# Softmax biases and part of P's high halves on ACT in place of DVE

## The chip, the core and the metric

The kernel runs on one core of a Trainium2 chip. The metric is the device time of one execution in microseconds (us); the figure given for a kernel is the median of its runs. A core has engines with instruction queues of their own, each worked off in order: PE (TensorE, matmuls; PEld is its weight load), DVE (VectorE), ACT (ScalarE), POOL (GpSimd) and SP (SyncE), which here issues most DMAs and all DMA transposes. Engines wait for each other by semaphores.

## What is computed

Three blocks, one after the other. Block-masked attention over 8 batches, 8 heads, 576 positions and a head width of 64; then a dense gated layer over its 4608 tokens; then a routed layer of 8 experts that each take the 576 tokens with the highest logits in one global greedy order.

```python
scores = scale * np.matmul(q, k.transpose(0, 1, 3, 2))
scores = np.where(block_i >= block_j, scores, -1000000000.0)   # blocks of 64
scores = scores - np.max(scores, axis=-1, keepdims=True)
attn = np.exp(scores)
attn = attn / (np.sum(attn, axis=-1, keepdims=True) + 1e-09)
x = np.matmul(attn, v)                       # then (B*S, H*D) = (4608, 512)
a, b = x @ w1, x @ w2                        # 512 -> 1024
x = (a * b @ w3) @ w_out                     # 1024 -> 512
...                                          # greedy assignment of tokens to experts
out[mask] = np.maximum(x[mask] @ w1[e], 0.0) @ w2[e]
```

The change touches the attention's softmax alone: the subtraction of the row maximum, which enters the exponential as a bias, and the division by the row sum.

## The kernel before

All matmuls keep about 32-bit precision by splitting a number into a high and a low fp16 half: the high half is the rounded product, the low half is what the rounding left. A product then takes three matmuls (high x high, high x low, low x high).

The attention is worked through in 32 steps n, one for each pair of heads of a batch. A step has four score tiles S in PSUM (two buffers), made by PE: `last` (L239, the last 64 rows of both heads, 576 keys), and three by `rows` and `mm` (L200, L204): query block 3 (512 keys, both heads), blocks 2 and 0 (384 and 128 keys, both heads), and block 1 (256 keys, both heads). Each tile goes through `finish`:

- DVE takes the row maxima of the scores (L213 for two heads at once, L215 for `last`) into `nb[:, 0]`.
- One DVE instruction multiplies them by minus the scale and writes the biases `nb[:, 1]` (L217; 1, 2 or 4 numbers per partition).
- ACT forms E = exp(scale x S + bias) and the row sums (L221), one instruction for each part.
- DVE turns the sums into reciprocals `rr` (L224, L225).
- For each part the high half of P = E x rr is written in fp16 (L229 on DVE or L231 on ACT), and DVE forms the low half (L232), which reads the high one.

So a step has four biases and nine parts: one of 576 keys and two each of 512, 384, 256 and 128. `N // P` is 4 for 576 and for 512 keys; `DVE_HI = (2, 3, 4)` puts the high halves of all but the 128-key parts on DVE. P lies in two SBUF tiles with one buffer each: P13 (`last` and block 3) and P12 (blocks 2, 0 and 1). SP transposes each by DMA into PT (L259), PE multiplies it with v (L276, `pv`), and ACT and DVE take the result out as xT (L280, L281).

Into these steps other work is woven, by the lists `fills`: the first dense layer's weights are decoded from 64-bit numbers and split in steps 1 to 7 (`decode`, L385 on ACT and L386 to L390 on DVE, then L126, L118, L119), w_out and w3 are prepared in steps 8 to 30, and 128 units of the dense layer (`moe_unit`: 24 matmuls at L301, ACT L306, DVE L311, a store by SP) begin with step 5, four a step. Then come the rest of the dense layer, the routing and the experts.

In the attention part the order on each engine is not that of the code: a scheduler that knows dependencies, buffers and a cost for every instruction lays all queues out when the kernel is built. An edit in one place can therefore move instructions elsewhere. The routing part has a fixed order.

Of the kernel before, what the change touches and what calls it, by code (L numbers as in the profile page):

```python
# [12 lines left out]
AF = mybir.ActivationFunctionType  # L13
ALU = mybir.AluOpType
# [15 lines left out]
R3 = 2  # L30
LE = 37
SW = 30
DVE_HI = (2, 3, 4)
TH = 5
TB = 15
TBX = 5
# [23 lines left out]
def moe_kernel(ctx, tc, q, k, v, moe_w1, moe_w2, moe_w3, moe_w_out, w_gate, ew1, ew2, out):  # L60
    nc = tc.nc
    P = 128
# [128 lines left out]
    def s_tiles(n):  # L191
        tq, tk, t4, c = qkT[n]
        pa_, pc_ = (x[n % PB] for x in Pb)

        def mm(ps, o, m):
            N = (m + 1) * P
            for a, b in PRODUCTS:
                for hh in range(2):
                    r = slice(64 * hh, 64 * hh + 64)
                    nc.tensor.matmul(ps[:, hh, o:o + N], tq[r, a, m * P:m * P + P], tk[r, b, :N],  # L200
                                     start=a + b == 0, stop=False)
            for hh in range(2):
                r = slice(64 * hh, 64 * hh + 64)
                nc.tensor.matmul(ps[:, hh, o + N - 64:o + N], hide[r], low[r], start=False, stop=True)  # L204

        def finish(ps, parts):
            nb = sm.tile([P, 3, 4], F32, name="nb", bufs=8)
            e = c2.tile([P, 2, 512], F32, name="E", bufs=3)
            ef, pf_ = (x.rearrange("p a b -> p (a b)") for x in (e, ps))
            k_ = 0  # L210
            for hh, o, N, _, _ in parts:
                if hh == 0:
                    nc.vector.tensor_reduce(nb[:, 0, k_:k_ + 2], ps[:, :, o:o + N], axis=AX.X, op=ALU.max)  # L213
                elif hh is None:
                    nc.vector.tensor_reduce(nb[:, 0, k_:k_ + 1], pf_[:, :N], axis=AX.X, op=ALU.max)  # L215
                k_ += 1
            nc.vector.tensor_scalar(nb[:, 1, :k_], nb[:, 0, :k_], c[:, 1:2], None, op0=ALU.mult)  # L217
            sums = sm.tile([P, 4], F32, name="sums", bufs=8)
            at = [slice((hh or 0) * 512 + o, (hh or 0) * 512 + o + N) for hh, o, N, _, _ in parts]
            for x, a in enumerate(at):  # L220
                nc.scalar.activation(ef[:, a], pf_[:, a], AF.Exp, bias=nb[:, 1, x:x + 1], scale=c[:, 0:1],  # L221
                                     accum_out=sums[:, x:x + 1])
            r = sm.tile([P, 2, 4], F32, name="rr", bufs=8)
            nc.vector.tensor_scalar(r[:, 0, :k_], sums[:, :k_], 1e-9, 2.0 ** -TS, op0=ALU.add, op1=ALU.mult)  # L224
            nc.vector.reciprocal(r[:, 1, :k_], r[:, 0, :k_])  # L225
            for x, (_, _, N, dst, b0) in enumerate(parts):
                hi, lo = (dst[:, z].rearrange("p b c -> p (b c)")[:, b0 * P:b0 * P + N] for z in range(2))
                if N // P in DVE_HI:
                    nc.vector.tensor_scalar(hi, ef[:, at[x]], r[:, 1, x:x + 1], None, op0=ALU.mult)  # L229
                else:  # L230
                    nc.scalar.activation(hi, ef[:, at[x]], AF.Copy, scale=r[:, 1, x:x + 1])  # L231
                nc.vector.scalar_tensor_tensor(lo, ef[:, at[x]], r[:, 1, x:x + 1], hi, op0=ALU.mult, op1=ALU.subtract)  # L232

        def last():
            ps = ps_s.tile([P, 2, 512], F32, name="S")
            pf_ = ps.rearrange("p a b -> p (a b)")
            for a, b in PRODUCTS:
                for k0, N in ((0, 512), (512, 64)):
                    nc.tensor.matmul(pf_[:, k0:k0 + N], t4[:, a], tk[:, b, k0:k0 + N], start=a + b == 0, stop=a == 1)  # L239
            finish(ps, [(None, 0, S, pa_, 0)])  # L240

        def rows(*ms):
            def f():
                ps = ps_s.tile([P, 2, 512], F32, name="S")
                parts, o = [], 0
                for m, dst, b0 in ms:
                    mm(ps, o, m)
                    parts += [(hh, o, (m + 1) * P, dst, b0 + hh * (m + 1)) for hh in range(2)]
                    o += (m + 1) * P
                finish(ps, parts)  # L250
            return f

        return [last, rows((3, pa_, 5)), rows((2, pc_, 0), (0, pc_, 6)), rows((1, pc_, 8))]
# [330 lines left out]
    for i in range(nl):  # L584
        n = max(n if i else 0, SW + int(i * (LE - SW) / nl), min(NS + 5, 8 + 2 * (i // 2)) if i % 2 else 0)
# [575 lines left out]
```

## Time and profile before

| | |
|---|---|
| median of 3 runs | 1585.56 us (1579.64 to 1587.46) |
| profiled execution, time | 1581.55 us |
| profiled execution, span from first to last instruction | 1579.8 us |
| busy over the span | PE 1366.2 us (86%), DVE 1077.4 us (68%), ACT 795.2 us (50%), POOL 98.3 us (6%) |
| mean granted TensorE clock | 0.945 of full speed |
| high halves on DVE (L229) | 224 instructions; on ACT (L231) 64 of 128 keys |
| biases (L217) | 128 instructions on DVE |

The shares are means over stages that differ: the attention fills the span from about 13 us to about 757 us. DVE is at 90% or more of a slice in most of the first 500 us, PE from then on. The chain of work that ended last, followed back from the end, reaches only to about 1143 us, so it says nothing of the attention; that has to be read from the busy times by stage and from the waits of each engine. A row of waits names the engine and line that waited, what it was let go by, the total in us, how often, and the longest.

### The profile page before, as it was taken

What the parts mean: (1) busy time and instruction counts of PE and PEld (TensorE: products, weight loads), DVE (VectorE), ACT (ScalarE), POOL (GpSimd) and SP (SyncE); (2) the same over time, 40 slices, a digit from 0 to 9 for tenths busy, and PEclk for the clock granted to TensorE, in tenths of its full rate; (3) what the DMA queues carried; (4) which work ended last, traced back from release to release, by engine and by line L of the source; (5) the groups of instructions that cost most, each with busy time, mean ns of one, the idle gap of its engine ahead of it and who ended that gap; (6) DMA issues with size and microseconds to landing.
All of it is one profiled execution on the core that took longest, in us unless ns stands there. A gap on an engine that the chain in (4) does not pass through costs nothing. (4 is left out here: it accounts for less than half of the span.)

```text
span 1579.8 us, 32788 instructions
## 1 busy us (share of the span) xinstructions
PE 1366.2 (86%) x12811; PEld 934.5 (59%) x12811; DVE 1077.4 (68%) x3308; ACT 795.2 (50%) x1881; POOL 98.3 (6%) x136
## 2 busy tenths in 40 slices
PE   3547888789899999999998898879768999999997
PEld 2335656466566666666666665656556656556663
DVE  8999999879888988886115888878743353333610
ACT  7766676566666656544312333353314564655611
POOL 0000000000000000010200000000024121200101
PEclk7559999999999999999999999989879999999999
DMA  7768797887858865559955324332358663642200
GB/s 247 182 148 197 137 232 168 172 200 149 194 136 201 175 169 108 121 114 282 286 172 186 101 81 135 100 120 94 101 112 190 181 199 134 152 149 74 80 27 34
DMA packets 379658, 238.57 MB, mean 151 GB/s; under 512 B 261232, under 2 KB 344688, under 8 KB 378480
## 3 DMA queue, kind: packets, MB, share of 16 engines
q1 hardware_dynamic: 372064, 215.47, 54.2%
q0 software_dynamic: 5760, 18.90, 3.8%
q8 instruction: 100, 1.64, 0.4%
q10 hardware_dynamic: 1680, 2.11, 0.4%
q14 instruction: 54, 0.44, 0.1%
HBM read 132.61 MB, written 39.86 MB: 109 GB/s over the span
## 5 line engine op out<-in xcount | busy, mean ns | idle before, releaser
L301 PE MATMUL ab<-xT,w1h 128*128 128x288 f16 x1536 | 217.6, 290 | 9.0 <-ACT a_sb L306 8.6
L301 PE MATMUL ab<-xT,w2h 128*128 128x288 f16 x1536 | 218.1, 290 | 6.5 <-ACT a_sb L306 2.8
L221 ACT ACTIVATE E<-S,nb,cc 128x128 f32<-128x128 f32 (+4 forms) x288 | 181.2, 639 | 78.3 <-DVE nb L217 52.5
L1079 PE MATMUL pe<-xT,ewa 128*128 128x288 f16 (+2 forms) x1728 | 198.4, 279 | 15.0 <-DMA xT<-xg 10.1
L1079 PEld LDWEIGHTS <-ewa 128*128 128x128 f16 x1728 | 161.2, 101 | 50.8 <-issue 15.4
L1096 PE MATMUL pe<-ewb,h 128*128 128x512 f16 (+1 forms) x960 | 189.1, 379 | 0.0
L301 PEld LDWEIGHTS <-w2h 128*128 128x128 f16 x1536 | 146.3, 100 | 56.1 <-issue 15.8
L301 PEld LDWEIGHTS <-w1h 128*128 128x128 f16 x1536 | 144.8, 99 | 58.3 <-issue 19.3
L276 PE MATMUL PV<-PT,v 128*64 128x128 f16 (+1 forms) x2880 | 100.1, 223 | 66.6 <-DMA PT<-P 55.6
L232 DVE SCALAR_TENSOR_TENSOR P<-E,rr,P 128x128 f16<-128x128 f32 (+4 forms) x288 | 157.3, 572 | 0.4
L1096 PEld LDWEIGHTS <-h 128*128 128x128 f16 (+1 forms) x960 | 85.4, 101 | 99.0 <-issue 2.6
L276 PEld LDWEIGHTS <-v 128*64 128x64 f16 x2880 | 85.1, 118 | 91.0 <-issue 50.6
L1082 DVE SCALAR_TENSOR_TENSOR h<-pe,h 128x288 f16<-128x288 f32 (+2 forms) x144 | 57.1, 420 | 107.6 <-ACT h L1081 107.5
L922 PE MATMUL px<-W34l,gh 128*128 128x512 f32 x288 | 123.6, 429 | 0.0
L922 PE MATMUL px<-W34h,gh 128*128 128x512 f32 x288 | 122.4, 425 | 0.2 <-ACT gh L937 0.2
L922 PE MATMUL px<-W34h,gl 128*128 128x512 f32 x288 | 122.4, 425 | 0.0
L311 DVE SCALAR_TENSOR_TENSOR g<-ab,vr,a_sb 128x288 f32<-128x288 f32 x124 | 65.6, 529 | 69.6 <-PE ab L301 47.5
L306 ACT ACTIVATE a_sb<-ab 128x288 f32<-128x288 f32 x128 | 52.4, 409 | 119.5 <-PE ab L301 111.2
L937 ACT ACTIVATE gh<-g 128x1024 fp32r<-128x1024 f32 x36 | 38.1, 1059 | 142.3 <-PE px L922 135.1
L1081 ACT ACTIVATE h<-pe 128x288 f16<-128x288 f32 (+2 forms) x144 | 52.1, 380 | 108.5 <-PE pe L1079 108.1
L213 DVE TENSOR_REDUCE nb<-S 128x2 f32<-128x1024 f32 (+3 forms) x128 | 101.3, 814 | 4.8 <-PE S L204 4.8
L229 DVE TENSOR_SCALAR P<-E,rr 128x384 f16<-128x384 f32 (+3 forms) x224 | 88.0, 429 | 1.6
(279 smaller groups left out, 2158.6 us busy)
## 6 DMA issues: line engine op xcount, KB each, us to landing
g<-gd SPq DMA_DIRECT2D x36, 512.0 KB, 3.7
gd<-g SPq DMA_DIRECT2D x62, 288.0 KB, 3.4
g<-gd SPq DMA_DIRECT2D x15, 1152.0 KB, 7.6
raw<-in_moe_w_dram SPq DMA_DIRECT2D x32, 512.0 KB, 4.9
esa<-in_moe_w_dram SPq DMA_DIRECT2D x8, 2048.0 KB, 9.2
esb<-in_moe_w_dram SPq DMA_DIRECT2D x8, 2048.0 KB, 8.4
v<-in_v_dram SPq DMA_DIRECT2D x8, 1280.0 KB, 6.9
xr<-row SPq DMA_DIRECT2D x36, 256.5 KB, 3.3
```

The costliest lines, as they stand in the source:

```text
L213: nc.vector.tensor_reduce(nb[:, 0, k_:k_ + 2], ps[:, :, o:o + N], axis=AX.X, op=ALU.max)
L221: nc.scalar.activation(ef[:, a], pf_[:, a], AF.Exp, bias=nb[:, 1, x:x + 1], scale=c[:, 0:1], accum_out=sums[:, x:x + 1])
L229: nc.vector.tensor_scalar(hi, ef[:, at[x]], r[:, 1, x:x + 1], None, op0=ALU.mult)
L232: nc.vector.scalar_tensor_tensor(lo, ef[:, at[x]], r[:, 1, x:x + 1], hi, op0=ALU.mult, op1=ALU.subtract)
L276: nc.tensor.matmul(ps[hh * 64:hh * 64 + 64, c0:c0 + w], vt[:, zv, hh, j, :], s, start=z == 0 and j == 0, stop=z == 2 and j == nj - 1)
L301: nc.tensor.matmul(p[:, :288], w[:, zw, cc, :], x[:, zx, cc, c0:c0 + 288], start=first, stop=cc == 3 and zw == 1)
L306: nc.scalar.activation(a, p[:, :288], AF.Copy, scale=2.0 ** -15)
L311: nc.vector.scalar_tensor_tensor(g, ps["w2"][:, :288], iv[b][:, f:f + 1], a, op0=ALU.mult, op1=ALU.mult)
L922: nc.tensor.matmul(p, gh[a][:, f], W34[b][:, f], start=f == 0 and a + b == 0, stop=f == 7 and a == 1)
L1079: nc.tensor.matmul(p[:, :n], w1[:, a, cc, f * P:(f + 1) * P], t[:, 4 * b + cc, x], start=cc == 0 and a + b == 0, stop=cc == 3 and a == 1)
L1082: nc.vector.scalar_tensor_tensor(h[:, 1, f, x], p[:, :n], 0.0, h[:, 0, f, x], op0=ALU.max, op1=ALU.subtract)
L1096: nc.tensor.matmul(p[r0:r1], h[:, a, f, k_ * P + r0:k_ * P + r1], EW[e, "b"][0][:, b, f], start=f == 0 and a + b == 0, stop=f == 7 and a == 1)
```

## The change

`DVE_HI` becomes two lists, one for steps 0 to 7 and one for steps 8 to 31, and the bias instruction goes from DVE to ACT:

```diff
-DVE_HI = (2, 3, 4)
+DVE_HI = (2,), (2, 3)
...
-            nc.vector.tensor_scalar(nb[:, 1, :k_], nb[:, 0, :k_], c[:, 1:2], None, op0=ALU.mult)
+            nc.scalar.activation(nb[:, 1, :k_], nb[:, 0, :k_], AF.Copy, scale=c[:, 1:2])
...
-                if N // P in DVE_HI:
+                if N // P in DVE_HI[n >= 8]:
                     nc.vector.tensor_scalar(hi, ef[:, at[x]], r[:, 1, x:x + 1], None, op0=ALU.mult)
                 else:
                     nc.scalar.activation(hi, ef[:, at[x]], AF.Copy, scale=r[:, 1, x:x + 1])
```

In each of steps 0 to 7 five high halves go to ACT (one of 576, two of 512, two of 384 keys), in each of steps 8 to 31 three (576, 512, 512). That is 40 + 72 = 112 of the 224, and all 128 biases. The scheduler lays all queues out anew; three places show how.

ACT in step 2 before, where E_653 (576 keys) and E_673 (512) are the exponentials of P13, dec, wd and wp belong to the decoding of weights, and P130 is P13:

```order
L221 ACTIVATE E_653,sums_656<-S_645,nb_652,cc_471 128x576
L118 ACTIVATE w2h1_80<-wd_872,wp_883 128x512
L126 ACTIVATE w1h2_72,wm_1005<-wd_998 128x512
L221 ACTIVATE E_673,sums_676<-S_663,nb_672,cc_471 128x512 x2
L280 ACTIVATE xT_320<-PV_567 128x192
L118 ACTIVATE qkT_977<-qk32_500,qp_982 128x1152 x2
```

The same place of ACT now:

```order
L126 ACTIVATE w2h2_81,wm_1147<-wd_1140 128x512
L385 ACTIVATE dec_1260<-raw_1016 128x512
L385 ACTIVATE dec_1405<-raw_1159 128x512
L221 ACTIVATE E_653,sums_656<-S_645,nb_652,cc_471 128x576
L280 ACTIVATE xT_320<-PV_567 128x192
L217 ACTIVATE nb_672<-nb_672,cc_471 128x2
L221 ACTIVATE E_673,sums_676<-S_663,nb_672,cc_471 128x512 x2
L231 ACTIVATE P130_119<-E_653,rr_658 128x576
L217 ACTIVATE nb_768<-nb_768,cc_471 128x4
L118 ACTIVATE w1h2_72<-wd_998,wp_1009 128x512
L118 ACTIVATE w2h2_81<-wd_1140,wp_1151 128x512
L231 ACTIVATE P130_119<-E_673,rr_679 128x512 x2
```

The high halves stand behind the next exponentials or behind weight splits, and two decodes, which wait for a DMA of raw weights, now stand ahead of E_653.

DVE in the same step before, around the high half of E_653:

```order
L224 TENSOR_SCALAR rr_679<-sums_676 128x2
L229 TENSOR_SCALAR P130_119<-E_653,rr_658 128x576
L281 SCALAR_TENSOR_TENSOR xT_320<-PV_567,xT_320 128x192
L390 SCALAR_TENSOR_TENSOR wd_1140<-raw_891,dec_1141 128x512
L213 TENSOR_REDUCE nb_768<-S_751 128x2 x2
```

And now, from a reciprocal of E_673 to the low half of E_653:

```order
L225 RECIPROCAL rr_679<-rr_679 128x2
L84 TENSOR_SCALAR wp_1151<-wp_1151 128x1
L416 COPY w2i_87<-wp_1151 128x1
L418 SCALAR_TENSOR_TENSOR iw12_88<-w1i_78,wp_1151 128x1
L232 SCALAR_TENSOR_TENSOR P130_119<-E_653,rr_658,P130_119 128x576
```

The L229 between reciprocal and low half is gone, and the low half L232 now waits for ACT's L231.

ACT in step 10 before, where a_sb belongs to units of the dense layer:

```order
L306 ACTIVATE a_sb_3483<-ab_3470 128x288
L221 ACTIVATE E_3363,sums_3366<-S_3355,nb_3362,cc_3142 128x576
L306 ACTIVATE a_sb_3564<-ab_3551 128x288
L221 ACTIVATE E_3383,sums_3386<-S_3373,nb_3382,cc_3142 128x512 x2
L306 ACTIVATE a_sb_3687<-ab_3674 128x288
```

And now:

```order
L217 ACTIVATE nb_3362<-nb_3362,cc_3142 128x1
L221 ACTIVATE E_3242,sums_3245<-S_3232,nb_3241,cc_2349 128x256 x2
L221 ACTIVATE E_3363,sums_3366<-S_3355,nb_3362,cc_3142 128x576
L306 ACTIVATE a_sb_3338<-ab_3325 128x288
L118 ACTIVATE qkT_3848<-qk32_3160,qp_3853 128x1152 x2
L231 ACTIVATE P130_119<-E_3363,rr_3368 128x576
L217 ACTIVATE nb_3382<-nb_3382,cc_3142 128x2
L280 ACTIVATE xT_2887<-PV_3267 128x192
L221 ACTIVATE E_3383,sums_3386<-S_3373,nb_3382,cc_3142 128x512 x2
L306 ACTIVATE a_sb_3413<-ab_3400 128x288
L217 ACTIVATE nb_3529<-nb_3529,cc_3142 128x4
L231 ACTIVATE P130_119<-E_3383,rr_3389 128x512 x2
```

Biases and high halves lie between exponentials and the evacuations of dense units (the units beside a given step are earlier ones now: a_sb_3413 where a_sb_3687 stood).

## Rows read from the trace of the kernel before

**Rows 1.** Busy time by stage: start:end, length, us (instructions) per engine, clock, DMA share.
```profile
core 0: us, PE busy (x) PEld busy (x) DVE busy (x) ACT busy (x) POOL busy (x), PEclk, DMA share, GB/s
13.00:192.50 179.50, 109.50 (x1322) 77.95 (x1318) 171.91 (x506) 122.37 (x299) 0.00 (x0) 0.75 0.75 178
192.50:450.90 258.40, 221.69 (x2609) 156.93 (x2610) 233.09 (x620) 165.18 (x403) 0.00 (x0) 0.97 0.82 182
450.90:757.00 306.10, 289.68 (x3411) 199.72 (x3409) 250.82 (x670) 167.93 (x420) 6.09 (x13) 0.99 0.71 164
```

**Rows 2.** L217 alone in these stages: length, DVE us (instructions), clock, DMA share, GB/s.
```profile
13.00:192.50 179.50, 6.89 (x32) 0.75 0.75 178
192.50:450.90 258.40, 9.31 (x44) 0.97 0.82 182
450.90:757.00 306.10, 10.88 (x52) 0.99 0.71 164
```

**Rows 3.** Waits of DVE from 13 to 192.5 us, the longest in total.
```profile
DVE rr L224 <- ACT E L221: 2.3, 4, 1.3
```

**Rows 4.** Waits of PE from 13 to 192.5 us.
```profile
PE PV L276 <- DMA PT<-P: 33.8, 17, 7.2
PE S L200 <- ACT E L221: 10.7, 10, 3.3
```

**Rows 5.** Waits of SP's DMA queue from 13 to 192.5 us.
```profile
SPq L259 <- DVE P L229: 45.1, 15, 7.5
```

**Rows 6.** Waits of PE from 192.5 to 450.9 us.
```profile
PE PV L276 <- DMA PT<-P: 15.4, 16, 2.0
PE S L239 <- ACT E L221: 7.4, 4, 3.4
PE lgp L469 <- DMA w3h<-wo: 4.9, 4, 2.0
```

**Rows 7.** Waits of PE from 450.9 to 757 us.
```profile
PE PV L276 <- DMA PT<-P: 6.5, 7, 1.9
```

**Rows 8.** Waits of ACT from 13 to 192.5 us.
```profile
ACT dec L385 <- DMA raw<-in_moe_w_dram: 17.0, 9, 4.0
ACT xT L280 <- PE PV L276: 11.0, 5, 3.9
ACT E L221 <- DVE wp L80: 7.3, 3, 4.4
```

**Rows 9.** Instructions by line and shape: count, busy us, mean ns, idle before.
```profile
L229 DVE TENSOR_SCALAR P<-E,rr 128x512 f16<-128x512 f32 x64 | 28.0, 479 | 0.5
L229 DVE TENSOR_SCALAR P<-E,rr 128x384 f16<-128x384 f32 x64 | 24.1, 419 | 0.6
L231 ACT ACTIVATE P<-E,rr 128x128 f16<-128x128 f32 x64 | 22.4, 406 | 4.9 <-issue 2.4 <-DVE rr L225 1.5 <-DVE rr L224 1.0
L229 DVE TENSOR_SCALAR P<-E,rr 128x576 f16<-128x576 f32 x32 | 16.4, 513 | 0.4
```

**Rows 10.** Line L118: ns of one (least/median/most), first and last start.
```profile
L118 ACT ACTIVATE w1h<-wd,wp x8: 715/726/762, 32.7 to 172.0; 128x512 f16<-128x512 f32 x8
L118 ACT ACTIVATE wgxh<-wg,wgxp x1: 326/326/326, 280.2 to 280.2; 128x32 f16<-128x32 f32 x1
```

**Rows 11.** Instructions in order of time, 75 to 99 us: start, us, engine, instruction.
```profile
85.53 0.22 DVE L217 TENSOR_SCALAR nb<-nb,cc 128x2 f32<-128x2 f32 x1
85.66 0.75 DVE L386 TENSOR_SCALAR dec<-dec 128x512 f32<-128x512 f32 x2
...
94.17 0.87 DVE L229 TENSOR_SCALAR P<-E,rr 128x512 f16<-128x512 f32 x2
94.24 0.72 ACT L118 ACTIVATE w2h<-wd,wp 128x512 f16<-128x512 f32 x1
...
94.85 0.56 ACT L221 ACTIVATE E<-S,nb,cc 128x256 f32<-128x256 f32 x1
...
94.96 0.44 DVE L167 TENSOR_SCALAR vr<-iw,vs 128x1 f32<-128x1 f32 x2
```

## The prediction, made before the changed kernel ran

> **What bounds the kernel now.** I read the busy time by stage first, then each engine's waits inside a stage, then what single instructions cost. I cut the attention at the first reduce of steps 0, 8 and 19 and at its end, so that the three stages hold 8, 11 and 13 steps (32, 44 and 52 biases, four a step) [rows 2].
>
> In the first stage, 13.0 to 192.5 us, DVE is busy 171.9 of 179.5 us; ACT has 122.4 and PE 109.5 [rows 1]. The longest total wait of DVE there is 2.3 us, for a row sum [rows 3], so DVE is simply full. What PE waits for most is the transposed P, 33.8 us [rows 4]; and SP, which issues those transposes, waits 45.1 us for DVE's part of P [rows 5]. So PE's wait for PT is largely a wait for DVE, passed on by a DMA.
>
> In the second stage, to 450.9 us, no engine is full: of 258.4 us DVE has 233.1 (90%), PE 221.7 (86%), ACT 165.2 (64%) [rows 1]. PE still waits for PT, 15.4 us, then for exponentials that hold a score buffer, 7.4, and for the transposes of w3 and w_out, 4.9, with which the change has nothing to do [rows 6].
>
> In the third stage, to 757 us, PE is busy 289.7 of 306.1 us [rows 1]. Its longest wait, again for PT, is 6.5 us [rows 7]. What lies behind 757 us has no instruction of the change; I expect its time to stay.
>
> **What the change takes from DVE.** An instruction in a row of others costs less than its own duration, since the next begins before it ends. The bias lasts 0.22 us but the next DVE instruction starts 0.13 us after it (85.53 to 85.66); two high halves of 512 keys begin at 94.17 and what follows begins at 94.96, which is 0.395 each against a duration of 0.479 [rows 9, 11]. With the same 0.08 off, 576 keys cost 0.43 and 384 keys 0.335 [rows 9].
>
> - Steps 0 to 7: 0.43 + 2 x 0.395 + 2 x 0.335 + 4 x 0.13 = 2.41 us a step, 19.3 us in eight.
> - Steps 8 on: 0.43 + 2 x 0.395 + 4 x 0.13 = 1.74 us a step, 19.1 us in the second stage, 22.6 in the third.
>
> **What it gives to ACT.** A scaled copy of 512 numbers from fp32 to fp16 lasts 0.72 us on ACT and the next instruction starts 0.61 us after it (94.24 to 94.85); one of 128 lasts 0.406, so about 0.30 by the same 0.11 [rows 9 to 11]. On a straight line 384 keys cost 0.51 and 576 cost 0.66. No row shows a bias on ACT. The nearest is a scaled copy of 32 numbers, 0.326 us, so 0.22 in a row of others [rows 10]; the lower end is what it cost on DVE, 0.13, the upper 0.33 where the exponential right behind must wait for the whole of it. I take 0.22, the nearest row. Below nothing it can go too: the exponential then follows its bias on its own engine, and some of ACT's waits for a late DVE, such as the 7.3 us that exponentials waited in the first stage [rows 8], would shrink.
>
> - Steps 0 to 7: 0.66 + 2 x 0.61 + 2 x 0.51 + 4 x 0.22 = 3.78 us a step, 30.2 in eight.
> - Steps 8 on: 0.66 + 2 x 0.61 + 4 x 0.22 = 2.76 us a step, 30.4 in the second stage, 35.9 in the third.
>
> The bounds of the bias move the first of these sums by 32 x 0.1 = 3 us either way. [...]
>
> **First stage.** DVE falls to 171.9 - 19.3 = 152.6 us of work and ACT rises to 122.4 + 30.2 = 152.6: the two meet. Neither can be full all the time, since they now hand work to and fro: DVE makes the reciprocal, ACT the high half, DVE the low half. That ACT can take high halves without standing idle is shown by the 128-key ones that it has already: 64 of them had 4.9 us of idle time before them [rows 9]; at that price the 40 moved ones add 3 us at most. What I do not expect to shrink are the 17.0 us in which ACT stood before a decode because raw weights were still on their way [rows 8]; the order even puts two decodes ahead of an exponential now. The 11.0 us that it waited for PV [rows 8] and the DVE waits I let the added work fill. So ACT sets the stage: 152.6 + 17.0 = 169.6 us against 179.5, a gain of 9.9. The ends are a loss (the second rival) and 19.3, DVE's whole relief.
>
> [...]
>
> **Second stage.** DVE 233.1 - 19.1 = 214.0, ACT 195.6, PE 221.7 of 258.4: DVE falls below PE. What can be won is the part of PE's idle 36.7 us that came from late P. I take half of DVE's relief, 9.5 us, between nothing and 19.1: PE would then be 89% busy, less than it reaches in the third stage.
>
> **Third stage.** PE bounds it; ACT at 203.8 of 306.1 us has room. I take 1 us, between nothing and the 6.5 of the PT wait.
>
> **Sum.** 9.9 + 9.5 + 1 = 20.4 us off the profiled execution's 1581.55 gives 1561.2; off the median of the runs, 1585.56, it gives 1565.2. I forecast 1563.
>
> **Rivals.**
>
> *No change: DVE was only the busiest.* PE's waits for PT end with a DMA, and the DMA engines are 75 to 83% busy in these stages [rows 1]; P and PT have one buffer each, so a step's P cannot run ahead of the last step's transposes. For it: PE's longest wait names the DMA. Against it: SP itself waited 45.1 us for DVE [rows 5]. DVE's relief would come back as DVE's waits for ACT, the time would move by some 4 us at most: 1578 to 1585.
>
> *Slower: ACT's queue becomes the bound in steps 0 to 7.* ACT's old idle time, 57.1 us in the first stage, stays because it is spent before instructions that wait while others, ready, stand behind them: decodes for DMAs, exponentials for maxima, now biases for maxima and high halves for reciprocals as well. From the point where more than 179.5 - 152.6 = 26.9 us of it stays, the stage is longer than before. If three quarters stay (42.8), it takes 195.4 us, 16 more; with nothing won later, the time is 1598. If all stays it is 30 more, 1612. For it: 17.0 us of these waits are for DMAs, and the order has decodes ahead of exponentials. Against it: the high halves already on ACT waited little, and waits for DVE are part of the 57.1.
>
> *Larger gain: all relief turns into time.* 19.3 + 19.1 + 6.5 = 44.9 us less: 1537. It needs DVE and ACT both near 95% in the first stage.
>
> **How the numbers follow.** Forecast 0.59, own range 1550 to 1576; no change 0.20; slower 0.14; larger gain 0.07. Half a per cent, about what a measurement of this kernel can tell from no change, is 7.9 us, so faster means under 1577.6. The forecast's own range and the larger gain lie there (0.65, and 0.01 of the no-change case): 0.66. Between the bounds I put the rest of the no-change case and the weak end of the forecast, 0.19; slower has 0.15, its own case and a little of the no-change one. The range, 1546 to 1592, leaves out most of the larger gain and the upper half of the slower case, some 0.14 together, and holds the bounds of the bias.
>
> **What would show it.** Right: step 8's first reduce comes about 10 us earlier, at 180 to 185 us, with ACT near 90% busy before it and DVE below 93%; the second stage is some 10 us shorter with PE near 89%; PE's wait for PT falls in both. The bias on ACT lasts about 0.3 us, the high halves 0.6 to 0.8. Wrong: step 8 begins later than 192.5 us with ACT waiting before L217 or L231, or DVE idle before L232 for the high half by as much as it was relieved; or the stages gain as said and the stage from 450.9 us gives it back, since PE there has 95% to do in any case.

## The result, and the profile after

The changed kernel takes 1590.88 us (median of 17 runs, 1586.78 to 1602.83), the kernel before 1583.36 (17 runs on the same chips): a ratio of 1.0064, 95% interval 1.0043 to 1.0085. It is slower by 0.6%, where 1563 us and a gain were forecast. The profiled execution took 1593.24 us, with a span of 1591.5.

The attention, cut as in [rows 1] at the first reduces of steps 0, 8 and 19 and at its end (start:end, length, then PE, PEld, DVE, ACT and POOL busy, clock, DMA share):

```profile
12.30:192.10 179.80, 112.71 (x1248) 77.95 (x1246) 162.19 (x450) 153.34 (x375) 0.00 (x0) 0.75 0.73 183
192.10:457.00 264.90, 229.20 (x2672) 162.08 (x2674) 211.50 (x524) 192.68 (x473) 0.00 (x0) 0.96 0.78 171
457.00:768.00 311.00, 289.49 (x3413) 202.03 (x3413) 228.71 (x580) 205.29 (x513) 5.92 (x13) 0.99 0.71 164
```

Against [rows 1] the stages changed by +0.3, +6.5 and +4.9 us, so the loss lies behind step 8; in the first stage the forecast gain of 9.9 is missing. The sums of work came about as worked out: ACT has 153.3 us in the first stage (forecast 152.6), DVE lost 21.6 and 22.1 us in the other two (19.1 and 22.6). DVE fell by 9.7 in the first, not 19.3, since the stage now holds other work too: DVE has 450 instructions there, 16 more than the 506 of before less the 72 moved ones, among them 20 of the weights' decode L386 where 18 stood.

PE's waits in the first stage (us in total, times, longest):

```profile
PE S L200 <- ACT E L221: 24.3, 13, 4.8
PE PV L276 <- DMA PT<-P: 16.5, 10, 4.7
PE S L239 <- ACT E L221: 9.4, 5, 3.2
```

The wait for PT halved from 33.8 [rows 4], as forecast, and SP's wait for DVE's high halves fell from 45.1 [rows 5] to 16.8, with 14 of them left on DVE where 54 were:

```profile
SPq L259 <- DVE P L229: 16.8, 5, 6.9
```

But all that SP waited before transposes (L259, whatever released it) hardly fell, from 90 to 84 us: other instructions took the place of DVE's high halves. And the score buffers came free late: L200's wait for an exponential, 10.7 before, is 24.3. DVE is no longer full, it stands 17.6 us; its longest waits are for ACT's decodes and for row sums (2.3 before [rows 3]):

```profile
DVE dec L386 <- ACT dec L385: 5.7, 5, 2.0
...
DVE rr L224 <- ACT E L221: 4.1, 6, 1.3
```

ACT's waits in the first stage shrank against [rows 8]: it is idle for 26.5 us (179.8 less 153.3) in place of 57.1. The decodes' wait for raw weights fell from 17.0 to 7.4, with 4.9 more for those of w_out; new is the bias's wait for its maximum:

```profile
ACT nb L217 <- DVE nb L213: 9.8, 6, 3.5
ACT dec L385 <- DMA raw<-in_moe_w_dram: 7.4, 5, 2.1
...
ACT dec L385 <- DMA raw<-in_moe_w_out_dram: 4.9, 2, 4.1
```

PE's wait for PT from 192.1 and from 457.0 us rose, against 15.4 [rows 6] and 6.5 [rows 7]:

```profile
PE PV L276 <- DMA PT<-P: 20.5, 14, 3.7
...
PE PV L276 <- DMA PT<-P: 8.8, 11, 1.8
```

The single high halves last 0.62 to 0.77 us, as expected, and a bias 0.29 (count, busy us, mean ns, idle before):

```profile
L231 ACT ACTIVATE P<-E,rr 128x512 f16<-128x512 f32 x64 | 42.5, 715 | 4.7 <-DVE rr L225 4.7
L231 ACT ACTIVATE P<-E,rr 128x576 f16<-128x576 f32 x32 | 24.6, 769 | 4.6 <-DVE rr L225 3.2 <-ACT E L221 1.2 <-ACT a_sb L306 0.2
L217 ACT ACTIVATE nb<-nb,cc 128x2 f32<-128x2 f32 x64 | 18.7, 293 | 36.0 <-DVE nb L213 35.9
L231 ACT ACTIVATE P<-E,rr 128x384 f16<-128x384 f32 x16 | 9.0, 619 | 0.0
```

So neither durations nor idle time before the moved high halves explain the loss. The idle time before the biases is long, 76.8 us over all three sizes, but it is old: before the change ACT stood 78.3 us ahead of the exponentials L221, now 2.8. The experiments ask what else explains it: the load on ACT, the hand-off between the engines, or the order of the queues.

### The profile page after: what moved, and what is told of

It reads as the page before. It is cut to its first block, busy times and chain, and to the rows that moved or that the text cites. A ratio compares the mean times of both kernels' runs of the same rounds, so it can differ in the third digit from the quotient of the medians.

```text
span 1591.5 us, 32778 instructions
## 1 busy us (share of the span) xinstructions
PE 1376.4 (86%) x12811; PEld 942.3 (59%) x12811; DVE 1024.5 (64%) x3068; ACT 891.7 (56%) x2121; POOL 98.0 (6%) x136
## 5 line engine op out<-in xcount | busy, mean ns | idle before, releaser
L301 PE MATMUL ab<-xT,w1h 128*128 128x288 f16 x1536 | 223.0, 295 | 11.5 <-ACT a_sb L306 11.3
L1079 PE MATMUL pe<-xT,ewa 128*128 128x288 f16 (+2 forms) x1728 | 198.6, 279 | 16.8 <-DMA xT<-xg 9.4
L221 ACT ACTIVATE E<-S,nb,cc 128x128 f32<-128x128 f32 (+4 forms) x288 | 181.1, 637 | 2.8 <-DVE P L232 0.9
L232 DVE SCALAR_TENSOR_TENSOR P<-E,rr,P 128x128 f16<-128x128 f32 (+4 forms) x288 | 155.7, 573 | 13.7 <-ACT P L231 11.9
L200 PE MATMUL S<-qkT 64*128 64x512 f16 (+3 forms) x768 | 83.7, 324 | 27.1 <-ACT E L221 26.3
L231 ACT ACTIVATE P<-E,rr 128x128 f16<-128x128 f32 (+3 forms) x176 | 97.2, 603 | 12.9 <-DVE rr L225 11.4
```

Source lines behind the costliest of these rows:

```text
L301: nc.tensor.matmul(p[:, :288], w[:, zw, cc, :], x[:, zx, cc, c0:c0 + 288], start=first, stop=cc == 3 and zw == 1)
L1079: nc.tensor.matmul(p[:, :n], w1[:, a, cc, f * P:(f + 1) * P], t[:, 4 * b + cc, x], start=cc == 0 and a + b == 0, stop=cc == 3 and a == 1)
```

## The experiments

Ratios are to the kernel before, run on the same chip between the others, with their 95% intervals; times of different runs are compared by these ratios (1% is 16 us), since the median of the kernel before goes from 1580.76 to 1585.23 us over the four chips of the experiments. "In the order of X" means: the order of each engine's queue is taken from kernel X and imposed by dependencies without a wait, so that all instructions the two have in common stand as in X; only those that differ are placed by the scheduler. In short:

```diff
+for eng, names in rows.items():          # the queues of the other kernel
+    last = None
+    for x in names:
+        if x in traced and str(traced[x].engine) == eng:
+            if last is not None:
+                tc.add_manual_dep(traced[x], last, DependencyInfo(NoSync, DATA))
+            last = x
```

### The two parts alone

e1_bias_only:

```diff
-DVE_HI = (2,), (2, 3)
+DVE_HI = (2, 3, 4), (2, 3, 4)
```

> Only the biases (L217) go to ACT; the high halves stay on DVE for the same sizes as before. Theory A (what ACT has to do makes it late with the exponentials, so that the score buffers come free late): the biases are 128 x 0.19 = 24 us of the 96 us that the change adds to ACT in all, a quarter, so a quarter of the loss of 7.5 us: about 1585, within 0.3% of before. Theory B (the order in which the scheduler lays the queues costs, whatever is moved): the order differs from before's in about as many places as the whole change's, so anything between 1575 and 1595, with no relation to the load.

Measured: 1549.77 us, ratio 0.9786 (0.9745 to 0.9827): the fastest kernel here that computes everything, 2.1% below before. Theory A missed by 35 us, and B's range by 25.

e2_hi_only, from the changed kernel:

```diff
-            nc.scalar.activation(nb[:, 1, :k_], nb[:, 0, :k_], AF.Copy, scale=c[:, 1:2])
+            nc.vector.tensor_scalar(nb[:, 1, :k_], nb[:, 0, :k_], c[:, 1:2], None, op0=ALU.mult)
```

> Only the high halves (512 and 576 keys, 384 in steps 0 to 7) go to ACT; the biases stay on DVE. Theory A: three quarters of the added ACT time and so most of the loss: 1588 to 1590. Theory B: anything between 1575 and 1595; were it under 1583, A would be hurt.

Measured: 1581.53, ratio 0.9997 (0.9963 to 1.0031): no change. The parts together lose what neither loses alone.

### Load against order

e3_after_in_order_before: the changed kernel's work, before's order.

> The changed kernel's work (biases and high halves on ACT), while every other instruction of each engine stands in the order that it has in the kernel before. Theory A: the load alone makes the loss, so 1588 to 1593, with step 8 at 191 to 194 us and the PE waits for E at L200 about as long as after's 24 us. Theory B: the loss goes, 1575 to 1584, and if the sum of the prediction holds for an unchanged order, down to 1563 with step 8 at 183.

Measured: 1603.85, ratio 1.0133 (1.0089 to 1.0178), step 8 at 195.5 us, and 17.6 us of PE waiting at L200 for E: slower than either theory said. The first stage takes 182.3 us, and DVE's longest wait in it is the one of its low halves for ACT's high halves:

```profile
13.20:195.50 182.30, 116.63 (x1330) 80.59 (x1327) 154.91 (x434) 151.19 (x370) 0.00 (x0) 0.78 0.74 175
...
DVE P L232 <- ACT P L231: 12.8, 8, 3.2
```

e4_before_in_order_after: the reverse.

> The work of the kernel before (biases and high halves on DVE), while every other instruction of each engine stands in the order that it has in the changed kernel. Theory A: about 1583, the time of before, since ACT has its old load. Theory B: 1590 or more, since the order is what costs, with step 8 at 192 or later.

Measured: 1617.81, ratio 1.0222 (1.0177 to 1.0268), step 8 at 201.6, as theory B has it. Both the work and the order cost: all of the change costs 1.3% in before's order (e3), and the changed kernel's order costs 2.2% with before's work (e4). An order that stays as it was would thus not have brought the forecast gain.

e5_bias_in_order_before: the biases on ACT, before's order.

> Only the biases on ACT, with every other instruction in the order of the kernel before. Theory A (the work: DVE is relieved of 128 x 0.19 = 24 us and ACT has room for as much): a gain remains without a new order, 1555 to 1575. Theory B (the 31 us that the first run gained come from the order that the scheduler laid for it): 1580 or more, since nothing but the place of 128 short instructions has changed.

Measured: 1572.64, ratio 0.9941 (0.9912 to 0.9969). Moving the biases is worth 0.6% in before's order; the rest of the first run's 2.1% came with its order. With the order kept, the 128 biases took 15.6 us off DVE's busy time in the three stages (655.8 to 640.2), 0.12 each and not the 0.19 of the estimate, and added 29.0 to ACT's (455.5 to 484.5), 0.23 each.

e6_after_in_order_bias: all of the change, in the order of e1.

> All of the change (biases and high halves on ACT), with every other instruction in the order of the kernel that has only its biases on ACT (1549.8 us). Theory A (the high halves' 72 us on ACT are too much): 1580 or more in that good order too. Theory B (the whole change only met a bad order): 1545 to 1560.

Measured: 1567.25, ratio 0.9884 (0.985 to 0.9918). The same instructions as in the changed kernel are 24 us faster (28 by the ratios), and faster than before: in this order the change gains, and that the changed kernel loses is due to its own order. Against e1 the high halves still cost 1.0%, 16 us by the ratios (17 by the medians).

### What the high halves cost in a fixed order

Three kernels in e1's order; the edits are shown in short, against e1's or e6's text. e7_bias_plus_load adds only the load:

```diff
                 if N // P in ((3, 4) if n < 8 else (4,)):
+                    nc.scalar.activation(idle[:, :N], ef[:, at[x]], AF.Copy, scale=r[:, 1, x:x + 1])
                     nc.vector.tensor_scalar(hi, ef[:, at[x]], r[:, 1, x:x + 1], None, op0=ALU.mult)
```

> The kernel with only its biases on ACT, its order kept, and ACT also forms the 112 high halves that the change moves, into a tile that nobody reads, while DVE forms the real ones as before: ACT's load of the change, without relief for DVE and without DVE's low halves waiting for ACT. Theory A1 (ACT's time alone is the loss): 1580 to 1600, about what all of the change takes in this order. Theory A2 (the loss is DVE's low half and the transfer waiting for ACT's high half): within 8 us of 1550.

Measured: 1557.39, ratio 0.9827 (0.9787 to 0.9868): the load costs 0.4% over e1, 6 us by the ratios (8 by the medians, on two chips). The two intervals overlap, so this is not clear of noise.

e8_bias_minus_hi only relieves DVE:

```diff
                 if N // P in ((3, 4) if n < 8 else (4,)):
-                    nc.vector.tensor_scalar(hi, ef[:, at[x]], r[:, 1, x:x + 1], None, op0=ALU.mult)
+                    if n == 0:
+                        nc.vector.tensor_scalar(hi, ef[:, at[x]], r[:, 1, x:x + 1], None, op0=ALU.mult)
```

> The kernel with only its biases on ACT, its order kept, without the 107 high halves for 512 and 576 keys (and 384 in steps 1 to 7) behind step 0: no engine forms them, so P's high halves there stay those of step 0. DVE is relieved of them and ACT gets nothing. If DVE's queue is still what the exponentials' biases and P wait for, as the prediction took it: 1525 to 1540. If DVE no longer sets anything: within 5 us of 1550.

Measured: 1537.89, ratio 0.97 (0.9671 to 0.973): the relief gains 0.9%, 14 us by the ratios (12 by the medians).

e9_after_in_order_bias_no_wait is e6 without DVE's wait for ACT: the 112 low halves subtract a tile of zeros.

```diff
-nc.vector.scalar_tensor_tensor(lo, ef[:, at[x]], r[:, 1, x:x + 1], hi, ...)
+nc.vector.scalar_tensor_tensor(lo, ef[:, at[x]], r[:, 1, x:x + 1], idle[:, :N], ...)
```

> All of the change in the order of the kernel with only its biases on ACT, which took 1567, but the 112 low halves whose high halves ACT forms subtract a tile of zeros, so that DVE needn't wait for ACT there (ACT forms the high halves all the same, and the transposes need them). Theory A2 (DVE, standing for ACT's high half, is the loss): 1545 to 1553, what DVE's relief (-12) and ACT's load (+8) leave of 1550. Theory A3 (the lateness of P for the transposes is the loss, whoever waits): 1562 or more.

Measured: 1553.69, ratio 0.9798 (0.9767 to 0.9829), against 0.9884 with the wait: DVE's standing for the high half costs 0.9%, 14 us. Load and relief alone would give 0.9786 + 0.0041 - 0.0086 = 0.9741; the 0.6% up to 0.9798 is left over. With an error of 0.3 to 0.4% on each ratio it is not clear of noise, and no run separates it (P's high half now comes from the other queue, and the transposes still need it). In the traces of e6 and e9 DVE and PE work in the same order up to 735 us, and ACT's order differs in 8 places. The stages say where the 14 us lie. First e1:

```profile
13.20:175.40 162.20, 103.83 (x1217) 71.98 (x1214) 160.85 (x459) 128.01 (x328) 0.00 (x0) 0.84 0.77 189
175.40:428.00 252.60, 228.23 (x2687) 161.62 (x2685) 228.88 (x587) 175.10 (x448) 0.00 (x0) 0.97 0.82 190
428.00:730.00 302.00, 291.26 (x3432) 202.47 (x3432) 241.98 (x622) 181.49 (x473) 6.08 (x13) 1.00 0.72 166
```

then e6, all of the change in that order:

```profile
12.80:175.80 163.00, 103.83 (x1214) 72.17 (x1211) 148.46 (x421) 148.01 (x362) 0.00 (x0) 0.72 0.77 189
175.80:434.00 258.20, 228.96 (x2691) 162.09 (x2691) 216.36 (x552) 195.72 (x487) 0.00 (x0) 0.97 0.83 186
434.00:747.20 313.20, 295.93 (x3434) 205.13 (x3435) 226.60 (x583) 205.43 (x512) 6.02 (x13) 0.98 0.69 161
```

and e9:

```profile
12.50:175.70 163.20, 103.46 (x1217) 72.78 (x1214) 148.50 (x421) 148.07 (x362) 0.00 (x0) 0.72 0.77 189
175.70:433.90 258.20, 227.55 (x2689) 161.45 (x2688) 216.40 (x552) 195.76 (x487) 0.00 (x0) 0.98 0.84 186
433.90:738.20 304.30, 291.14 (x3436) 202.54 (x3435) 226.69 (x583) 205.28 (x512) 6.08 (x13) 1.00 0.70 165
```

Of the stages only the third differs, by 8.9 us; of the 12.6 us between the two profiled executions the rest lies behind the attention, where the change has no instruction. In the third stage one wait of DVE stands out, in e6:

```profile
DVE P L232 <- ACT P L231: 22.7, 16, 2.7
```

and in e9, where two lines more make it L234 and L233:

```profile
DVE P L234 <- ACT P L233: 0.5, 1, 0.5
```

The stage in which ACT is only 66% busy is thus the one that the hand-off lengthens: taking DVE's wait away shortens it. Of the 8.9 us, PE is busy for 4.8 (its mean clock is 0.98 in place of 1.00) and idle for 4.1; no single wait of PE's grew by as much, so the way from DVE's wait to PE was not traced further.

### Why the changed kernel's own order is slow

e10_after_no_wait: the same edit in the changed kernel's own order.

> The changed kernel in its own order, with the same 112 low halves subtracting a tile of zeros instead of ACT's high half. In that order DVE stood only 12 us before low halves, so if DVE's standing is all that the hand-off costs: 1580 to 1590, and the rest of the loss lies in the order itself.

Measured: 1590.65, ratio 1.0037 (1.0016 to 1.0058), against 1.0064: the hand-off costs nothing here that is clear of noise (the scheduler put other work between reciprocal and low half, as in the queue of step 2 above). With the wait DVE stood 11.9 us before low halves in the three stages together, against 22.7 in e6's third alone. This kernel is also the changed one with its own order imposed on it; up to 735 us its trace shows the changed kernel's order on PE, DVE and ACT, and the time is the same, so imposing an order has no price of its own that shows.

e11_bias_in_order_after:

> Only the biases on ACT, with every other instruction in the order of the changed kernel. If the changed kernel's order is bad for any work (its weights decoded earlier, its dense units and PV later): 1570 to 1590, 20 or more above this work in its own order. If it is only bad together with ACT's high halves: below 1560.

Measured: 1597.31, ratio 1.0076 (1.0049 to 1.0104), above the 1570 to 1590 that were expected for a bad order: 3% or 46 us by the ratios over the same work in its own order. For before's work (e4) and for the biases the changed kernel's order is the slowest that was run; for the whole change before's order is slower still (e3).

e12_before_in_order_bias:

> The work of the kernel before, with every other instruction in the order of the kernel with only its biases on ACT. If that order is simply the better one: 1565 to 1575, 10 above the same order with the biases on ACT, as in the order of before. If an order fits only the work it was laid for: 1583 or more.

Measured: 1569.86, ratio 0.9903 (0.987 to 0.9937): without moving any work, the order alone gains 1%.

The orders of these four kernels, with the work that was run in them, as ratios to before. A kernel in its own order is the kernel as the scheduler laid it:

| work \ order of | before | e1 (biases) | changed | e2 (high halves) |
|---|---|---|---|---|
| before | 1 | 0.9903 | 1.0222 | |
| biases on ACT | 0.9941 | 0.9786 | 1.0076 | |
| high halves on ACT | | | | 0.9997 |
| both | 1.0133 | 0.9884 | 1.0064 | 0.9930 |

Down a column only the work changes: the biases on ACT gain 0.6 to 1.4% each time (from the third to the fourth row in the last column), the high halves cost 1.9 and 1.0% in two orders and nothing in the changed kernel's. Along a row only the order changes, by 2.5 to 3.2%: more than all of the change gains or loses in any one of them (-1.5 to +1.3%).

e13_after_in_order_hi:

> The whole change, with every other instruction in the order of the kernel that has only its high halves on ACT (1581.5 us in that order). If the changed kernel's own order is one unlucky draw: below 1580, by the 10 to 20 us that the biases gave in the other orders. If any order laid with the high halves on ACT is bad: 1585 or more.

Measured: 1572.52, ratio 0.993 (0.9903 to 0.9957): an order laid with the high halves on ACT need not be bad. Of the four orders in which all of the change ran, the changed kernel's own is the second slowest.

e14_after_ostep9 and e15_bias_ostep9:

```diff
-OSTEP = 8
+OSTEP = 9
```

> The changed kernel with the preparation of w_out one step later (step 9 in place of 8); the scheduler lays a new order, the work is the same. If orders scatter: away from 1591 by 5 us or more to either side, most of it up to step 19. If the loss belongs to the work: 1586 to 1596.

> The same date moved in the kernel with only its biases on ACT. If its 1550 was a lucky order: 1558 or more. If the gain belongs to the work: 1545 to 1557.

Measured: 1584.78, ratio 1.0016 (0.9995 to 1.0037), with the gain between steps 8 and 19 (255.2 us for 264.9); and 1568.9, ratio 0.9919 (0.9894 to 0.9943). A date moved by one step lays another order: 8 us better for the one and 21 worse for the other by the ratios (6 and 19 by the medians). More than half of e1's gain is gone with it: e1's order was a lucky one, though 1569 still beats before.

e16_after_one_chunk_later:

```diff
-WSTEP = {1: 2, 2: 2, 3: 2, 4: 2, 5: 2, 6: 3, 7: 3}
+WSTEP = {1: 1, 2: 2, 3: 2, 4: 2, 5: 3, 6: 3, 7: 3}
```

> The changed kernel with one of the two chunks of expert weights due in step 1 moved to step 5, so that less is prepared in the first four steps. If early weights ahead of the exponentials are the loss: step 8 at 178 to 186 us in place of 192, and 1575 to 1585. If not: step 8 at 190 or later, and any scatter of the whole is that of a new order.

Measured: 1575.65, ratio 0.9969 (0.9945 to 0.9993), step 8 at 187.2 us: the time is that of the first answer, step 8 lies between the two. Step 7 began 18 us earlier than in the changed kernel (155 for 173), but took 32.2 us for 19.1, with 343 matmuls for 196. The larger part of the gain lies in the second stage (252.1 us for 264.9), and the edit lays a new order too, so early weights are not shown to be the loss.

What stands ahead of the exponentials shows in ACT's queue at step 3 (start, us, instruction; rows of accumulators and, at the dots, of other instructions left out). The changed kernel, whose first reduce of that step starts at 74.6:

```profile
76.03 0.64 ACT L126 ACTIVATE w1h<-wd 128x512 f16<-128x512 f32 x1
...
77.25 0.30 ACT L217 ACTIVATE nb<-nb,cc 128x2 f32<-128x2 f32 x1
77.44 1.71 ACT L231 ACTIVATE P<-E,rr 128x384 f16<-128x384 f32 x4
79.03 0.67 ACT L385 ACTIVATE dec<-raw 128x512 f32<-128x512 f32 x1
...
79.77 0.66 ACT L385 ACTIVATE dec<-raw 128x512 f32<-128x512 f32 x1
80.31 1.37 ACT L118 ACTIVATE v<-v,vp 128x1280 f16<-128x1280 f32 x1
81.57 0.57 ACT L221 ACTIVATE E<-S,nb,cc 128x256 f32<-128x256 f32 x1
82.11 0.57 ACT L221 ACTIVATE E<-S,nb,cc 128x256 f32<-128x256 f32 x1
```

and e6, the same work, whose reduce starts at 73.7:

```profile
74.80 0.72 ACT L118 ACTIVATE w1h<-wd,wp 128x512 f16<-128x512 f32 x1
75.41 0.56 ACT L221 ACTIVATE E<-S,nb,cc 128x256 f32<-128x256 f32 x1
75.95 0.56 ACT L221 ACTIVATE E<-S,nb,cc 128x256 f32<-128x256 f32 x1
...
77.29 1.71 ACT L231 ACTIVATE P<-E,rr 128x384 f16<-128x384 f32 x4
78.89 0.84 ACT L221 ACTIVATE E<-S,nb,cc 128x576 f32<-128x576 f32 x1
```

In the changed kernel the last exponentials of step 2 come 7.0 us after step 3's reduce, behind four high halves, two decodes and parts of weights and of v; in e6 they come 1.7 us after it, ahead of these. ACT idles in neither piece. Step 3 takes 27.6 us in the one and 22.6 in the other, and it is as long in the other kernels with the changed kernel's order (27.6 in e11, 29.1 in e4). This piece is not all of the order's loss: it is 5 of the 16.8 us by which the first stages differ, and 6.7 more are lost in the second. Most of the first stage's difference lies in steps 4 to 6, the changed kernel first, with PE's wait for exponentials in each:

```profile
102.20:173.00 70.80, 52.84 (x592) 36.27 (x593) 61.83 (x177) 56.34 (x145) 0.00 (x0) 0.79 0.78 186
...
PE S L200 <- ACT E L221: 12.5, 5, 4.8
```

```profile
96.30:152.50 56.20, 39.88 (x500) 28.32 (x498) 53.49 (x150) 49.28 (x126) 0.00 (x0) 0.79 0.84 193
...
PE S L200 <- ACT E L221: 6.8, 5, 2.4
```

These 14.6 us are in part work that stands earlier: the changed kernel does more on every engine in these steps, and its step 7 is 4.2 us shorter. Free of such cuts, its attention takes 755.7 us and e6's 734.4. What in the order loses the 21 us was not traced further than this.

## Why the prediction was wrong

**That DVE bounds the first stage was right.** With the order kept, taking work from DVE shortens it (e8: 155.2 us against e1's 162.2), and the biases alone, in before's order, do so too (e5: 176.3 us against 179.5). First e8, then e5:

```profile
12.40:167.60 155.20, 100.58 (x1212) 70.95 (x1209) 149.31 (x426) 126.95 (x324) 0.00 (x0) 0.73 0.82 199
...
13.20:189.50 176.30, 111.35 (x1322) 77.62 (x1318) 167.77 (x473) 128.59 (x329) 0.00 (x0) 0.85 0.74 181
```

**First stage, "ACT sets the stage: 152.6 + 17.0 = 169.6 us". This is the step that failed, by its second term.** ACT's work came as worked out, 153.3 us. Its idle time was 26.5 us in place of 17.0, and these 9.5 us are nearly all of the missing gain of 9.9. The text let only the decodes' waits stay, which came to 12.3 us (7.4 and 4.9), and put the others at nothing; but the bias's wait for its maximum alone was 9.8 us. Nor does the work by itself fix the idle time. For the same work it was 31.1 us in before's order (e3, a stage of 182.3), 26.5 in the changed kernel's own and 15.0 in e1's (e6, a stage of 163.0 with DVE and ACT both 91% busy). The text saw two decodes ahead of an exponential and high halves behind weight splits, and gave them no price; nor did it price DVE's standing for the high half, 12.8 us in e3. The order that was laid anew is thus what parts the changed kernel from e6, but the order of before would not have saved the forecast either: e3 is slower still. The 16.8 us between the first stages (179.8 and 163.0) are 11.5 of ACT's idle time and 5.3 of ACT's work, which stands earlier in the changed kernel.

**Second stage, half of DVE's relief.** Not borne out: 264.9 us in the changed kernel, 264.8 in before's order (e3) and 258.2 in e1's, where before takes 258.4. The biases alone, in before's order, gain nothing here (e5: 258.8), and in e1's order the high halves lengthen the stage by 5.6 us (252.6 to 258.2).

**Third stage, 1 us gained since ACT "has room".** The sign was wrong. With the order fixed, the high halves lengthen it by 11.2 us (302.0 to 313.2), of which e9 gives 8.9 back when DVE need not wait. Room on an engine by its busy share is not room at the moment when another engine's queue stops for it: ACT is 66% busy in e6's third stage, and DVE stands 22.7 us there for ACT's high halves. In the changed kernel's own order that wait is short (6.2 us) and the stage still 4.9 us longer than before's; why was not traced.

**The sum.** -20.4 us was forecast; e6 shows -18 (ratio 0.9884), but its stages differ from before's by -16.5, -0.2 and +7.1 us where -9.9, -9.5 and -1 were forecast: that the total comes near is luck. The changed kernel shows +10 (1.0064).

**The rivals.** The slower one, ACT's queue as the bound in steps 0 to 7, named the right queue and the right sign (PE's wait for exponentials there went from 10.7 to 24.3 us), and its own turning point was all but met: it has the stage longer than before from 26.9 us of ACT's idle time on, and with 26.5 the stage came out even (179.8 for 179.5). It did not have the loss behind step 8. Of the signs of being wrong that the text lists none came as written: step 8's reduce came at 192.1 us, and DVE stood only 0.9 us before low halves in the first stage. By the size "no change" came as near: its upper end lies 6 us under the measured time, the slower rival's 1598 lies 7 us over. (The DMA share that this rival gives as 75 to 83% is 71 to 82% in [rows 1]; no number of the forecast uses it.)

**The slower engine.** A high half of 512 keys lasts 0.715 us on ACT where it took 0.479 on DVE [rows 9]. In e1's order the 112 moved high halves took 40.3 us off DVE's busy time in the three stages (631.7 in e1, 591.4 in e6) and added 64.6 to ACT's (484.6 and 549.2). Their time on ACT (e7, the load) costs 6 to 8 us of the whole, not clear of noise; the hand-off (e6 against e9) costs 14, which is. For the biases, instructions of four numbers at most, the slower engine was no loss: one lasts 0.29 us on ACT where it took 0.22 on DVE, and on ACT they gained in each of the four orders, 0.6 to 1.4%.

## What to carry to other kernels

Where a scheduler lays the queues, time the moved work in a fixed order as well, and in more than one: here an order was worth 3% with the same work, more than the edit, and the busy sums of the attention show little of it (the changed kernel and e6: PE 631.4 and 628.7 us, ACT 551.3 and 549.2, DVE 602.4 and 591.4, in 755.7 and 734.4). In this kernel it paid to move to the slower engine what it consumes itself (a bias before its exponential) rather than what the other engine waits for (a high half before its low half). Before giving an engine work because it has room, look at who stands until it is done, as DVE did for 22.7 us of e6's third stage.

## What the runs showed of the hardware

A bias on ACT lasts 0.29 us. In the changed kernel's trace the next instruction starts 0.19 after it where that is a high half (77.25 to 77.44), and 0.33 where it is the bias's own exponential (87.97 to 88.30), the upper end of the prediction's bounds; the 0.23 of busy time for each in before's order (e5) is close to the 0.22 that was taken. Two engines that hand work to and fro reached 91% of a stage each (e6), close to the 95% that the prediction's larger gain asked for. And the lower granted clock went with hardly a longer stage here: the first stage took 163.0 us at a mean clock of 0.72 in e6 and 162.2 at 0.84 in e1, with PE busy 103.8 us in both.
